# Attention probabilities left unscaled, 1/sum applied to the product with v, and transposes in two row tiles, in a fused attention, FFT, MLP and gate kernel

## The chip, the cores and the metric

The kernel runs on one core of one Trainium2 chip. The metric is the device time of one launch in microseconds (us); lower is better. The core's engines run side by side, each in its own order: PE (TensorE: matmuls, and PEld, its loads of the stationary operand), DVE (VectorE), ACT (ScalarE), POOL (GpSimd) and SP (SyncE, which here only issues DMAs). An instruction starts when the one before it on its engine has been issued and every semaphore that it waits for has come.

## The reference

Three blocks follow each other. The result of each is the x of the next.

```python
# 1: attention; batch 4, heads 8, seq 576, head_dim 64
scores = scale * q @ k.T
thresh = max(scores, -1) - tau                      # tau = 0.02
scores = where(scores >= thresh, scores, -1e9)
attn = exp(scores - max(scores))
attn = attn / (sum(attn, -1) + 1e-9)
x = attn @ v                                        # heads side by side: 4 x 576 x 512
# 2: mixing and MLP
u  = x + real(fft(fft(x, axis=1), axis=2))
un = (u - mean(u)) / sqrt(var(u) + 1e-6)
x  = u + relu(un @ w_ch1) @ w_ch2                   # 512 -> 2048 -> 512
# 3: gate
gate = sigmoid(causal depthwise convolution of x, 5 taps)
out = (gate * (x @ w_val)) @ w_out                  # 512 -> 512 -> 512
```

All inputs are 4-byte floats, except that the MLP and gate weights arrive as 8-byte words and are turned into two 4-byte parts each on the chip.

## The kernel before

**Attention.** Two heads form a head pair p; there are 16, and the 576 queries of the pair's two heads make nine tiles of 128 rows: four of each head (h = 0 or 1, i = 0 to 3) and one (h = 2) with the last 64 queries of both. So there are 144 tiles, numbered g, and 72 pairs of tiles, numbered u. One tile goes through these steps, each on one engine (`g_tile`):

- PE: scores `s` (L651). The head dimension is 64, so only half of the array's rows is needed: the upper 64 rows work out 288 keys and the lower 64 rows the other 288, as two *row tiles* whose matmuls run beside each other. Queries `qt` therefore lie twice, on partitions 0 to 63 and 64 to 127.
- DVE: minus the row maximum, `neg` (L716); once for two tiles the threshold `thr` (L661).
- ACT: the exponential `e` (L722).
- DVE: `p` (L733), which keeps the exponentials of scores over the threshold and sums them into `su`.
- ACT adds 1e-9 to the sums (L666) and DVE takes 1/sum (L668), once for two tiles; POOL multiplies `p` by it (L741).
- PE: four transposes of 128x128, `t` (L753), into one PSUM bank; there are two such banks (`ps_t`). The last 64 keys of each tile go through `g_tail` (L678, L682) into a bank of another pool.
- ACT: copies `t` to `m` (L770).

When a group of tiles of a pair is there, PE multiplies by v (L431, `f`), ACT copies the product to `xt` (L436), and the FFT's folds and matmuls follow after every fourth pair.

**Weights.** The MLP's weights come in 40 pieces of 128x512 words. POOL issues the loads into `raw` buffers (L903), then DVE (L261, L262, L265, L266, L267), ACT (L263, L264, L270) and POOL (L271) turn a piece into its high and low part. These conversions fill gaps of the attention and go on during the MLP's first chunk (chunk 0), in which `h` (L1216) and `c` (L1252) are the matmuls, ACT makes `hh` (L1228) and DVE `hl` (L1230). Chunks 1 to 4 (L1062, L1078) and the gate (L1450, L1468) follow.

**Order.** Nothing is ordered at run time. A planner in the program, `loom`, runs all these steps as generators against written costs (the second value of each `yield`, in ns), ranks (the third; a lower one is more urgent) and rooms (buffers), and emits each engine's instructions in the order that comes out of its own clock. A changed cost or rank thus moves instructions everywhere.

Of the kernel before, what the change touches and what calls it, by code (L numbers as in the profile page):

```python
# [32 lines left out]
GVF = 4  # L33
XB = 2
PBUFS = 6
# [7 lines left out]
HOLD = {"PE": 200.0, "DVE": 200.0, "ACT": 200.0, "POOL": 200.0}  # L43
# [7 lines left out]
SWAP = 350.0  # L51
# [25 lines left out]
class Loom:  # L77
# [222 lines left out]
def attention_fft(tc, right, ps_f, a, u_d, dram, conv_w, loom):  # L300
# [3 lines left out]
    with ExitStack() as right2, ExitStack() as right2b, ExitStack() as right3, ExitStack() as right4, ExitStack() as scores, ExitStack() as turned:  # L304
# [29 lines left out]
        ths = [[const.tile([128, n], F32, name=f"th{i}_{n}") for n in (256, 320)] for i in range(2)]  # L334
# [70 lines left out]
        def pt_tile(p, c):  # L405
            if (p, c) not in pt:
                pt[p, c] = (pt0_p, pt1_p)[c].tile([128, 2, 4, 256] if c == 0 else [128, 4, 640], F32, tag=f"m{c}", name=f"m{c}")
            return pt[p, c]

        def g_pv(p, c):  # L410
# [11 lines left out]
            for t in range(5):  # L422
# [217 lines left out]
        sc, neg, thr, ex, ssum, p_t = {}, {}, {}, {}, {}, {}  # L640
# [23 lines left out]
        def g_sum(u):  # L664
            yield "ACT", 210.0, 0.2
            ACT.activation(ssum[u], ssum[u], AF.Copy, bias=1e-9)  # L666
            yield "DVE", 155.0, 0.0
            DVE.reciprocal(ssum[u], ssum[u])  # L668
            loom.mark("r", u)

        def g_tail(p, rows):
            for j, i in enumerate(rows):
                yield ("PE", 112.0 if i < 4 else 120.0, 0.4, "full" if i < 4 else "col", *(["room"] if j == 0 else []))
                if j == 0:
                    f, room = fill_tile()
# [12 lines left out]
            ACT.activation(th[:, o:o + n], f[:, 0:n], AF.Copy)  # L688
# [3 lines left out]
        def g_tile(g):  # L692
            p, h, i = tiles[g]
            u, j = divmod(g, 2)
            c = 0 if i < 2 else 1
            yield "after", ("kq", p), *([("s", g - 1)] if g else []), *([("k", g - 2)] if g > 1 else [])
# [940 lines left out]
```

## Time and profile before

| what | value |
|---|---|
| median of 3 runs | 857.98 us (856.91 to 858.8) |
| the profiled execution: time, span of its instructions | 858.75 us, 857.0 us |
| mean granted TensorE clock, share of full speed | 0.992 |
| attention's loop: first `neg` to last `p` on DVE | 6.66 to 323.78 us |
| chunk 0 of the MLP: first `hl`, last `hl` on DVE; end of the chunk | 339.27, 434.73; 438.06 us |
| chunks 1 to 4 of the MLP | 438.06 to 751.05 us |
| gate and output | 751.05 us to the end |

The time of an execution is 1.75 us more than the span, which goes from its first instruction to its last. Busy times of different engines overlap, so they don't add up to the span. A stage is bound by the engine that is hardly idle in it, or by a chain that goes round several engines.

### The profile page before, as it was taken

What the parts mean: (1) busy time and instruction counts of PE and PEld (TensorE: products, weight loads), DVE (VectorE), ACT (ScalarE), POOL (GpSimd) and SP (SyncE); (2) the same over time, 40 slices, a digit from 0 to 9 for tenths busy, and PEclk for the clock granted to TensorE, in tenths of its full rate; (3) what the DMA queues carried; (4) which work ended last, traced back from release to release, by engine and by line L of the source; (5) the groups of instructions that cost most, each with busy time, mean ns of one, the idle gap of its engine ahead of it and who ended that gap; (6) DMA issues with size and microseconds to landing.
All of it is one profiled execution on the core that took longest, in us unless ns stands there. A gap on an engine that the chain in (4) does not pass through costs nothing.

```text
span 857.0 us, 13874 instructions
## 1 busy us (share of the span) xinstructions
PE 824.7 (96%) x4886; PEld 650.6 (76%) x4886; DVE 560.2 (65%) x1212; ACT 420.3 (49%) x855; POOL 384.7 (45%) x450
## 2 busy tenths in 40 slices
PE   6999999999999999999999999999999999999998
PEld 4555556656665656788889999998888788898986
DVE  6999999998988987797757632142123656328740
ACT  4877777787867765644545323133121331133432
POOL 3456974797588657574352431023003010075421
PEclk6999999999999999999999999999999999999999
DMA  7359455636754369959435622003000230532111
GB/s 213 101 155 244 131 144 155 190 121 208 203 168 144 102 205 334 376 197 365 151 124 179 212 65 60 0 28 108 1 1 12 93 105 1 194 122 90 62 50 62
DMA packets 63885, 117.37 MB, mean 137 GB/s; under 512 B 14658, under 2 KB 21826, under 8 KB 63816
## 3 DMA queue, kind: packets, MB, share of 16 engines
q1 hardware_dynamic: 56280, 92.62, 33.9%
q0 software_dynamic: 7104, 23.57, 9.0%
q8 instruction: 39, 0.64, 0.3%
q10 hardware_dynamic: 432, 0.30, 0.1%
q14 instruction: 30, 0.25, 0.1%
HBM read 84.99 MB, written 31.47 MB: 136 GB/s over the span
## 4 chain that ended last, share of the span: by engine, by line
PE 62%; DVE 17%; POOL 6%; issue 6%; ACT 5%; DMA 3%; SPq 0%; DVEq 0%; POOLq 0%; ACTq 0%
PE c L1078 15%; PE h L1062 14%; DVE neg L716 6%; DVE p L733 5%; PE o L1468 5%; PE h L1216 5%; PE v L1450 5%; PE s L651 5%; PE c L1252 4%; PE f L431 4%; PE t L753 3%; ACT e L722 2%; POOL p L741 2%; POOL res L1087 1%; PE f L563 1%
## 5 line engine op out<-in xcount | busy, mean ns | idle before, releaser
L741 POOL TENSOR_SCALAR p<-p,su 128x576 f32<-128x576 f32 x144 | 111.6, 784 | 89.2 <-DVE su L668 76.8
L1066 DVE SCALAR_TENSOR_TENSOR hl<-h,hh 128x384 fp32r<-128x384 f32 (+1 forms) x64 | 39.8, 622 | 147.4 <-ACT hh L1065 145.7
L1065 ACT ACTIVATE hh<-h 128x384 fp32r<-128x384 f32 (+1 forms) x64 | 34.8, 544 | 200.7 <-PE h L1062 195.5
L722 ACT ACTIVATE e<-s,neg 128x576 f32<-128x576 f32 x144 | 103.7, 741 | 51.4 <-DVE neg L716 38.7
L733 DVE SCALAR_TENSOR_TENSOR p<-s,thr,e 128x576 f32<-128x576 f32 x144 | 113.3, 815 | 11.2 <-ACT e L722 2.6
L716 DVE TENSOR_REDUCE neg<-s 128x1 f32<-128x576 f32 x144 | 103.1, 747 | 11.1 <-PE s L651 10.1
L651 PE MATMUL s<-kt,qt 64*128 64x288 f32 (+1 forms) x640 | 100.7, 448 | 8.5 <-DVE p L733 5.9
L1078 PE MATMUL c<-hl,w1h 128*128 128x384 f32 (+1 forms) x256 | 92.9, 363 | 1.9 <-DVE hl L1066 1.9
L1078 PE MATMUL c<-hh,w1h 128*128 128x384 f32 (+1 forms) x256 | 92.6, 362 | 0.0
L1078 PE MATMUL c<-hh,w1l 128*128 128x384 f32 (+1 forms) x256 | 92.6, 362 | 0.0
L753 PE MATMUL t<-ident,p 128*128 128x128 f32 x536 | 83.9, 286 | 8.3 <-POOL p L741 4.0
L753 PEld LDWEIGHTS t<-ident,p 128*128 128x128 f32 x536 | 59.4, 143 | 38.3 <-POOL p L741 24.7
L651 PEld LDWEIGHTS s<-kt,qt 64*128 64x128 f32 (+1 forms) x640 | 47.2, 179 | 46.9 <-issue 19.7
L770 ACT ACTIVATE m<-t 128x512 f32<-128x512 f32 x134 | 76.1, 600 | 12.6 <-PE t L753 12.2
L431 PE MATMUL f<-m,v 128*64 128x320 f32 (+1 forms) x512 | 72.4, 413 | 0.9 <-ACT th L688 0.9
L1062 PE MATMUL h<-unh,w0h 128*128 128x384 f32 (+1 forms) x256 | 61.6, 362 | 0.0
L1062 PE MATMUL h<-unh,w0l 128*128 128x384 f32 (+1 forms) x256 | 61.6, 362 | 0.0
L1062 PE MATMUL h<-unl,w0h 128*128 128x384 f32 (+1 forms) x256 | 61.5, 362 | 0.0
L1087 POOL TENSOR_TENSOR res<-ht,res 128x512 f32<-128x512 f32 (+1 forms) x20 | 23.0, 1188 | 84.2 <-DVE ht L1086 84.2
L431 PEld LDWEIGHTS f<-m,v 128*64 128x64 f32 x512 | 32.7, 136 | 29.3 <-issue 8.7
L1078 PEld LDWEIGHTS c<-hl,w1h 128*128 128x128 f32 x256 | 48.1, 188 | 7.9 <-DVE hl L1066 2.9
L1078 PEld LDWEIGHTS c<-hh,w1l 128*128 128x128 f32 x256 | 48.0, 188 | 5.0
(262 smaller groups left out, 1676.6 us busy)
## 6 DMA issues: line engine op xcount, KB each, us to landing
raw<-in_moe_w_ch POOLq DMA_DIRECT2D x32, 512.0 KB, 6.1
qt<-in_q SPq DMA_DIRECT2D x30, 288.0 KB, 6.9
kt<-in_k SPq DMA_DIRECT2D x15, 432.0 KB, 4.6
ypad<-y_d SPq DMA_DIRECT2D x16, 288.0 KB, 4.4
out<-os SPq DMA_DIRECT2D x18, 256.0 KB, 2.0
v<-in_v SPq DMA_DIRECT2D x16, 256.0 KB, 3.1
e_h<-cx SPq DMA_DIRECT2D x16, 256.0 KB, 2.4
e_l<-ct SPq DMA_DIRECT2D x16, 256.0 KB, 2.1
```

The costliest lines, as they stand in the source:

```text
L431: PE.matmul(out=f[h * 64:h * 64 + 64, 0:n], lhsT=w, rhs=r, start=(t == 0), stop=(t == 4))
L651: PE.matmul(out=s[o, c, 0:HALF], lhsT=qt[w, hh, q], rhs=kt[w, 2 if h == 2 and hh else hh], start=True, stop=True)
L716: DVE.tensor_reduce(out=neg[u][:, j, 0:1], in_=sc[g][:, :, 0:HALF], axis=AX.XY, op=ALU.max, negate=True)
L722: ACT.activation(e, sc[g][:, :, 0:HALF], AF.Exp, bias=neg[u][:, j, 0:1], scale=1.0)
L733: DVE.scalar_tensor_tensor(out=p_view(g).rearrange("p (a b) -> p a b", a=2), in0=sc.pop(g)[:, :, 0:HALF], scalar=thr[u][:, j:j + 1], in1=e ...
L741: POOL.tensor_scalar(out=v, in0=v, scalar1=ssum[u][:, j:j + 1], scalar2=1.0, op0=ALU.mult, op1=ALU.mult)
L753: PE.matmul(out=f[:, t, :], lhsT=pv[:, t * 128:(t + 1) * 128], rhs=ident, is_transpose=True, start=(t == 0), stop=(t == 3))
L770: ACT.activation(o, fv, AF.Copy)
L1062: PE.matmul(out=f[:, 0:n], lhsT=ww[:, k * 128:(k + 1) * 128], rhs=x[:, k, 0:n], start=(i == 0), stop=(i == 3 * KB - 1))
L1078: PE.matmul(out=ch[c][o][:, 0:n], lhsT=ww[:, o * 128:(o + 1) * 128], rhs=x, start=(at_ == 0 and i == 0), stop=(at_ == FB - 1 and i == 2))
L1216: PE.matmul(out=f[:, 0:n], lhsT=ww[:, k * 128:(k + 1) * 128], rhs=x[:, k, 0:n], start=(i == 0), stop=(i == 3 * KB - 1))
L1450: PE.matmul(out=f[:, 0:HALF], lhsT=w[:, k, o * 128:(o + 1) * 128], rhs=x[:, k, s], start=(i == 0), stop=(i == 3 * KB - 1))
```

## The change

- `p` stays unscaled. The sums of a head pair go into one column block `ssum[p % 3]` of [128, 9]. Per pair three times (two rows of tiles, two more, the last) `g_tail` adds 1e-9 on ACT, takes 1/sum on DVE (48 reciprocals in place of 72), spreads it over 64 columns a head on POOL (`lt`, 32 copies and 16 multiplications of a constant), and turns it on PE beside the tails (64 transposes of 128x128 and 32 matmuls with `both`, all new). `th` is twice as wide: the tails, and 1/sum along the free axis. After ACT's copy of the product with v, POOL multiplies `xt` by the second half of `th`, 32 times. POOL's 144 multiplications of `p` are gone.
- The transposes of a tile are 8 matmuls of 64 rows (two row tiles) in place of 4 of 128 rows; those of two tiles follow each other into one `ps_t` buffer of two banks, of which there is one. `PBUFS`, the buffers of `p`, go from 6 to 5.
- `q` is written twice in DRAM (128 rows), so that one plain DMA on one queue loads it; the first pair's queries no longer go through ACT's queue. Two constants, `half` and `both`, are made on DVE ahead of the loop; `both` needs `ident` to be there.
- One more `raw` buffer for weights (`mlp_raw_top0`) from the stage "probs" on; the gate takes its four buffers from a list of the older ones.
- The planner's numbers: ROOMS, TURN, COPY, HOLD of ACT, SWAP, and the rank 1.2 for `g_unit`.

```diff
+TURN = 250.0
+COPY = 1.05
+ROOMS = {"room_t": 1}
...
-PBUFS = 6
+PBUFS = 5
...
-HOLD = {"PE": 200.0, "DVE": 200.0, "ACT": 200.0, "POOL": 200.0}
+HOLD = {"PE": 200.0, "DVE": 200.0, "ACT": 400.0, "POOL": 200.0}
-SWAP = 350.0
+SWAP = 300.0
...
-        ps_t = pool(turned, "ps_t", 2, space=PSUM)
+        ps_t = pool(turned, "ps_t", 1, space=PSUM)
+        ssum = [const.tile([128, 9], F32, name=f"su{i}") for i in range(3)]
-        ths = [[const.tile([128, n], F32, name=f"th{i}_{n}") for n in (256, 320)] for i in range(2)]
+        ths = [[const.tile([128, 2, n], F32, name=f"th{i}_{n}") for n in (256, 320)] for i in range(2)]
...
-            for j, q in enumerate((SP, second)):
-                q.dma_start(out=qt[j * 64:j * 64 + 64], in_=a["q"][b, n])
+            second.dma_start(out=qt, in_=a["q"][b, n])
...
+                yield "POOL", pool_ns(n), 0.3, "port"
+                POOL.tensor_tensor(out=x, in0=x, in1=th[:, 1], op=ALU.mult)
                 loom.mark("x", p, c)
...
-        def g_sum(u):
-            yield "ACT", 210.0, 0.2
-            ACT.activation(ssum[u], ssum[u], AF.Copy, bias=1e-9)
-            yield "DVE", 155.0, 0.0
-            DVE.reciprocal(ssum[u], ssum[u])
+        def g_tail(p, rows):
+            tail = rows[0] == 4
+            su = ssum[p % 3][:, 8:9] if tail else ssum[p % 3][:, 2 * rows[0]:2 * rows[0] + 4]
             yield "ACT", 210.0, 0.2
+            ACT.activation(su, su, AF.Copy, bias=1e-9)
+            yield "DVE", 155.0, 0.1
+            DVE.reciprocal(su, su)
+            yield "POOL", 250.0 if tail else 400.0, 0.1, "port"
+            lt = tmp_p.tile([128, 4, D], F32, tag="lt", name="lt", bufs=1)
+            if tail:
+                POOL.tensor_scalar(out=lt[:, 0:2], in0=half, scalar1=su, scalar2=1.0, op0=ALU.mult, op1=ALU.mult)
+            else:
+                POOL.tensor_copy(out=lt, in_=su.unsqueeze(2).to_broadcast([128, 4, D]))
...
+                for h in range(2):
+                    w = slice(h * 64, h * 64 + 64)
+                    PE.matmul(out=f[w, 64:128], lhsT=lt[:, h], rhs=both, start=True, stop=True)
...
+                for j in range(2):
+                    PE.transpose(f[:, 256 + j * 128:384 + j * 128], lt[:, 2 * j:2 * j + 2].rearrange("q h d -> q (h d)"), ident)
...
-            yield "after", ("r", u), *([("n", g - 1)] if g else [])
-            yield "POOL", 782.0, 0.1, "port"
-            v = p_view(g)
-            POOL.tensor_scalar(out=v, in0=v, scalar1=ssum[u][:, j:j + 1], scalar2=1.0, op0=ALU.mult, op1=ALU.mult)
-            yield "PE", 437.0, 0.5, "full", "room_t", "room"
+            gs = (g - 1, g) if h == 1 else (g,)
+            yield "PE", TURN * len(gs), 0.5, "row", "room_t"
...
-            for t in range(4):
-                PE.matmul(out=f[:, t, :], lhsT=pv[:, t * 128:(t + 1) * 128], rhs=ident, is_transpose=True, start=(t == 0), stop=(t == 3))
+                for t in range(4):
+                    for b in range(2):
+                        w = slice(b * 64, b * 64 + 64)
+                        PE.matmul(out=f[:, b, 4 * x + t], lhsT=pv[w, t * 128:(t + 1) * 128], rhs=ident[w, w], is_transpose=True, start=True, stop=True)
...
+        DVE.tensor_tensor(out=both, in0=ident[:, 0:D], in1=ident[:, D:128], op=ALU.add)
...
+                more_room("raw", "mlp_raw_top0", top)
```

In the instructions' order on each engine the following moves. Conversions whose last DVE step (L267, of the change L270) stands ahead of the attention's last `p`: 15 before, 5 with the change; from there to the first `hl`: 2 and 2; from the first `hl` to the last: 16 and 26; behind the last `hl`: 8 and 8. Of the single steps ahead of the last `p`, L261 goes from 16 to 7, L262 from 15 to 7, L265 and L266 from 15 to 6, L267 from 15 to 5, the reciprocals from 71 to 45. A `p` is followed by the next `neg` with no other instruction between them, or only a reciprocal, 20 times before and 54 times with the change.

DVE in the attention, with the `p` of the 53rd and 54th of the 144 tiles at the top, before (`p` is L733, `neg` L716):

```order
L733 SCALAR_TENSOR_TENSOR p,su<-s,thr,e 128x576 x2
L261 TENSOR_SCALAR cx<-raw 128x512
L668 RECIPROCAL su<-su 128x2
L262 TENSOR_SCALAR ct<-raw 128x512
L716 TENSOR_REDUCE neg_188<-s 128x1 x2
L661 TENSOR_REDUCE thr<-neg_188 128x2
L733 SCALAR_TENSOR_TENSOR p,su<-s,thr,e 128x576 x2
```

The same engine ten tiles on, around the `p` of the 65th and 66th tile, with the change (`p` is L751 now, `neg` L734):

```order
L734 TENSOR_REDUCE neg_190<-s 128x1
L676 RECIPROCAL su_181<-su_181 128x4
L734 TENSOR_REDUCE neg_190<-s 128x1
L667 TENSOR_REDUCE thr<-neg_190 128x2
L751 SCALAR_TENSOR_TENSOR p,su_182<-s,thr,e 128x576 x2
L734 TENSOR_REDUCE neg_191<-s 128x1 x2
L667 TENSOR_REDUCE thr<-neg_191 128x2
```

Where steps of a conversion stood between `p` and the next `neg`, often nothing stands there now. They stand in chunk 0 instead; DVE there, between two `hl` (L1230), before:

```order
L1230 SCALAR_TENSOR_TENSOR hl<-h,hh 128x512
L265 SCALAR_TENSOR_TENSOR cx<-raw,cx 128x512
L266 SCALAR_TENSOR_TENSOR raw<-raw,ct 128x512
L267 TENSOR_SCALAR raw<-cx 128x512
L261 TENSOR_SCALAR cx<-raw 128x512
L262 TENSOR_SCALAR ct<-raw 128x512
L1230 SCALAR_TENSOR_TENSOR hl<-h,hh 128x512
```

And with the change (`hl` is L1245; L264, L265, L268, L269 and L270 are the steps of a conversion):

```order
L1245 SCALAR_TENSOR_TENSOR hl<-h,hh 128x512
L264 TENSOR_SCALAR cx<-raw 128x512
L265 TENSOR_SCALAR ct<-raw 128x512
L264 TENSOR_SCALAR cx<-raw 128x512
L265 TENSOR_SCALAR ct<-raw 128x512
L268 SCALAR_TENSOR_TENSOR cx<-raw,cx 128x512
L269 SCALAR_TENSOR_TENSOR raw<-raw,ct 128x512
L270 TENSOR_SCALAR raw<-cx 128x512
L268 SCALAR_TENSOR_TENSOR cx<-raw,cx 128x512
L269 SCALAR_TENSOR_TENSOR raw<-raw,ct 128x512
L270 TENSOR_SCALAR raw<-cx 128x512
L1245 SCALAR_TENSOR_TENSOR hl<-h,hh 128x512
```

One conversion stood between these two `hl` before (elsewhere two), and with the change two stand between nearly all of them. PE in the attention, before (`t` is L753, `s` L651):

```order
L651 MATMUL s<-kt,qt 128x288 x2
L651 MATMUL s<-kt,qt 64x288 x4
L753 MATMUL t<-ident,p 128x128 x4
L563 MATMUL f<-csh,aeh 128x290
L678 MATMUL f<-ident,p 128x128 x2
L753 MATMUL t<-ident,p 128x128 x4
```

And with the change (`t` is L766, `s` L657, the turned 1/sum L698):

```order
L657 MATMUL s<-kt,qt 64x288 x4
L766 MATMUL t<-ident,p 128x64 x16
L657 MATMUL s<-kt,qt 128x288 x2
L556 MATMUL f<-sdh,xoh 95x256 x2
L556 MATMUL f<-sdl,xoh 95x256 x2
L696 MATMUL f<-ident,p 128x128 x2
L698 MATMUL f<-ident,lt 128x128 x2
```

Four transposes of 128 columns became eight of 64 for a tile, and those of two tiles stand together, beside scores, which use row tiles too.

## Rows read from the trace of the kernel before

**Rows 1.** The page's first part: busy time of each engine, share, instructions.

```profile
PE 824.7 (96%) x4886; PEld 650.6 (76%) x4886; DVE 560.2 (65%) x1212; ACT 420.3 (49%) x855; POOL 384.7 (45%) x450
```

**Rows 2.** Windows: us, busy (count) of PE, PEld, DVE, ACT, POOL, PEclk, DMA share, GB/s.

```profile
6.66:323.78 317.12, 297.59 (x2164) 186.81 (x2161) 286.95 (x691) 236.34 (x513) 216.04 (x274) 0.98 0.58 166
323.78:438.06 114.28, 110.71 (x557) 89.14 (x556) 88.85 (x135) 59.98 (x114) 61.99 (x70) 1.00 0.74 262
438.06:751.05 312.99, 311.10 (x1552) 279.72 (x1552) 131.87 (x241) 85.76 (x149) 59.32 (x55) 1.00 0.25 81
```

**Rows 3.** Attention, DVE by line: count | busy, mean ns | idle before, ended by.

```profile
L716 DVE TENSOR_REDUCE neg<-s 128x1 f32<-128x576 f32 x144 | 103.1, 747 | 11.1 <-PE s L651 10.1
L266 DVE SCALAR_TENSOR_TENSOR raw<-raw,ct 128x512 f32<-128x512 uint32 x14 | 11.7, 833 | 0.0
L668 DVE RECIPROCAL su<-su 128x2 f32<-128x2 f32 x71 | 11.2, 157 | 1.9 <-ACT su L666 1.7
L265 DVE SCALAR_TENSOR_TENSOR cx<-raw,cx 128x512 int32<-128x512 int32 x14 | 10.7, 767 | 0.0
L261 DVE TENSOR_SCALAR cx<-raw 128x512 int32<-128x512 int32 x15 | 7.9, 529 | 0.0
L262 DVE TENSOR_SCALAR ct<-raw 128x512 int32<-128x512 int32 x15 | 7.1, 474 | 0.0
L267 DVE TENSOR_SCALAR raw<-cx 128x512 int32<-128x512 int32 x14 | 6.2, 442 | 0.0
```

**Rows 4.** Timeline of DVE at 121.3 us: start, duration, instruction [idle before].

```profile
121.30 0.82 DVE L733 SCALAR_TENSOR_TENSOR p<-s,thr,e 128x576 f32<-128x576 f32 x1
...
122.05 0.81 DVE L733 SCALAR_TENSOR_TENSOR p<-s,thr,e 128x576 f32<-128x576 f32 x1
...
123.07 0.76 DVE L716 TENSOR_REDUCE neg<-s 128x1 f32<-128x576 f32 x1 [0.20 <-PE s L651]
```

**Rows 5.** First chunk, 323.78 to 438.06 us, DVE by line.

```profile
L265 DVE SCALAR_TENSOR_TENSOR cx<-raw,cx 128x512 int32<-128x512 int32 x18 | 16.1, 894 | 1.4 <-ACT cx L263 1.4
L266 DVE SCALAR_TENSOR_TENSOR raw<-raw,ct 128x512 f32<-128x512 uint32 x18 | 14.8, 820 | 0.3 <-ACT ct L264 0.3
L262 DVE TENSOR_SCALAR ct<-raw 128x512 int32<-128x512 int32 x18 | 14.5, 805 | 0.0
L261 DVE TENSOR_SCALAR cx<-raw 128x512 int32<-128x512 int32 x17 | 12.2, 717 | 0.9 <-ACT w0h L270 0.9
L267 DVE TENSOR_SCALAR raw<-cx 128x512 int32<-128x512 int32 x18 | 8.0, 446 | 0.0
```

**Rows 6.** Timeline of DVE: the first and the last `hl` of the 16 of chunk 0.

```profile
339.27 0.69 DVE L1230 SCALAR_TENSOR_TENSOR hl<-h,hh 128x512 fp32r<-128x512 f32 x1 [4.86 <-ACT hh L1228]
...
434.73 0.69 DVE L1230 SCALAR_TENSOR_TENSOR hl<-h,hh 128x512 fp32r<-128x512 f32 x1 [2.61 <-ACT hh L1228]
```

**Rows 7.** Timelines of DVE and of POOL in chunk 0, two stretches.

```profile
412.40 0.42 DVE L261 TENSOR_SCALAR cx<-raw 128x512 int32<-128x512 int32 x1
...
416.97 1.27 DVE L262 TENSOR_SCALAR ct<-raw 128x512 int32<-128x512 int32 x1
...
416.87 1.08 POOL L271 TENSOR_TENSOR w1l<-raw 128x512 fp32r<-128x512 f32 x1 [1.48 <-issue]
```

**Rows 8.** Timeline of PE at 105.5 us, then PE's weight loads of the attention by line.

```profile
105.55 1.09 PE L753 MATMUL t<-ident,p 128*128 128x128 f32 x8
106.57 1.24 PE L651 MATMUL s<-kt,qt 64*128 64x288 f32 x8
...
L753 PEld LDWEIGHTS t<-ident,p 128*128 128x128 f32 x528 | 58.5, 143 | 37.8 <-POOL p L741 24.7 <-issue 11.5 <-POOL xf L487 0.5
L651 PEld LDWEIGHTS s<-kt,qt 64*128 64x128 f32 x504 | 43.0, 191 | 39.7 <-issue 17.5 <-PE f L431 5.9 <-DVE p L733 4.4
```

**Rows 9.** The tile `ident`, 0 to 20 us: its load (duration ns, first and last start).

```profile
L786 SPq DMA_DIRECT2D ident<-in_ident x1: 590/590/590, 2.5 to 2.5; - x1
...
DMA to landing us min/median/max: 4.9/4.9/4.9
```

More of the change, by code (lines that the diff above doesn't have):

```diff
@@ L146, in start @@
         s = max(self.now[e], t.ready)
-        rooms = [(x, self.put.get(x, 0) - 2) for x in how if x.startswith("room")]
+        rooms = [(x, self.put.get(x, 0) - ROOMS.get(x, 2)) for x in how if x.startswith("room")]
         if rooms:
@@ L683, in g_tail @@
             for i in rows:
                 loom.mark("tailed", p, i)
-            o, n = (256, 64) if rows[0] == 4 else (0, 256)
             th = ths[p % 2][0 if rows[0] == 0 else 1]
-            yield "ACT", act(n), 0.3
-            ACT.activation(th[:, o:o + n], f[:, 0:n], AF.Copy)
+            o = 256 if tail else 0
+            yield "ACT", act(2 * n), 0.3
+            ACT.activation(th[:, :, o:o + n], f[:, 0:2 * n].rearrange("k (a q) -> k a q", a=2), AF.Copy)
             loom.free(room)
@@ L695, in g_tile @@
             c = 0 if i < 2 else 1
+            if g % 9 == 0 and p > 2:
+                yield "after", ("tailed", p - 3, 4)
             yield "after", ("kq", p), *([("s", g - 1)] if g else []), *([("k", g - 2)] if g > 1 else [])
@@ L711, in g_tile @@
                 if u >= 6:
-                    yield "after", ("n", 2 * u - 11)
-                thr[u], ssum[u] = (sm_p.tile([128, 2], F32, tag=nm, name=nm) for nm in ("thr", "su"))
+                    yield "after", ("k", 2 * u - 11)
+                thr[u] = sm_p.tile([128, 2], F32, tag="thr", name="thr")
             neg[u] = negs[u % len(negs)]
@@ new lines, in g_tile @@
+            m = pt_tile(p, c)
+            f, room = ps_t.tile([128, 2, 8, 64], F32, tag="t", name="t"), loom.room("room_t")
+            for x, y in enumerate(gs):
+                pv = p_view(y)[:, TAIL if tiles[y][1] == 1 else 0:]
+                for t in range(4):
+                    for b in range(2):
+                        w = slice(b * 64, b * 64 + 64)
+                        PE.matmul(out=f[:, b, 4 * x + t], lhsT=pv[w, t * 128:(t + 1) * 128], rhs=ident[w, w], is_transpose=True, start=True, stop=True)
+                loom.mark("t", y)
@@ L796, in attention_fft @@
                 DVE.tensor_copy(t[:, j, 1:2], atau)
+        half = const.tile([128, 2, D], F32, name="half")
+        both = const.tile([128, D], F32, name="both")
+        for h in range(2):
+            for x in range(2):
+                DVE.memset(half[x * 64:x * 64 + 64, h], float(x == h))
+        DVE.tensor_tensor(out=both, in0=ident[:, 0:D], in1=ident[:, D:128], op=ALU.add)
         loom.end = 8500.0
@@ L842, in mlp @@
         heads = [0, 0]
-        raws, spare = {}, {"raw": deque(), "cv": deque()}
+        raws, spare, kept = {}, {"raw": deque(), "cv": deque()}, set()
         at, loaded = [0], [0]
@@ L871, in used @@
         def used(j):
-            if more and nxt[0] + nxt[1] < FB:
+            if more and nxt[0] + nxt[1] < FB and all(ids[j, i] in stored for i in range(2)):
                 gone.append(j)
@@ L1098, in g_unit @@
             yield "after", *l0
-            yield "ACT", act(n), 3
+            yield "ACT", act(n), 1.2
             ACT.activation(uh[:, k, 0:n], z[:, k], AF.Copy)
-            yield "DVE", dve(n), 3, "port"
+            yield "DVE", dve(n), 1.2, "port"
             DVE.tensor_tensor(out=ul[:, k, 0:n], in0=z[:, k], in1=f32(uh[:, k, 0:n]), op=ALU.subtract)
@@ L1316, in start_gate @@
         def start_gate():
-            rooms = [spare["raw"].popleft() for _ in range(KB)]
+            rooms = [r for r in spare["raw"] if r in kept]
+            assert len(rooms) == KB
             ypad0 = [f32(r[0].tile([128, 512, 2], I32, tag="raw", name="ypad").rearrange("p a b -> p (a b)"))[:, 0:S + NK - 1] for r in rooms]
@@ L1605, in laid_out @@
     q, k, v = (x.reshape(B, NP, 2, S, D) for x in (q, k, v))
-    c = {"q": q.transpose(0, 1, 4, 2, 3).reshape(B, NP, D, 2, S)}
+    c = {"q": np.tile(q.transpose(0, 1, 4, 2, 3), (1, 1, 2, 1, 1))}
     k = np.stack([k[:, :, 0], np.roll(k[:, :, 1], TAIL, axis=-2), k[:, :, 1]], axis=2)
```

85 lines of the change are left out of this document (36 added, 49 removed).

## The prediction

> **What bounds the kernel now.** I read the page's busy shares first: PE is busy for 96% of the span, no other engine for more than 76% [rows 1]. That is a mean over stages, so the windows come next [rows 2]. In chunks 1 to 4 PE is busy 311.10 of 312.99 us, and in the gate stage, which the change's code leaves alone, nothing is gained either. In the attention PE is busy 297.59 of 317.12 us and DVE 286.95, both close to the whole, so neither alone sets the pace: the chain goes round scores, maximum, exponential, `p`. In chunk 0 PE is busy 110.71 of 114.28 us, DVE 88.85.
>
> Then DVE's groups in the attention [rows 3]: beside the maxima (0.747 us each) stand five steps of the weights' conversions and 71 reciprocals. What idle time `neg` meets is mostly PE's scores, 10.1 us in all. The timeline shows a pair of tiles: two `p` start 0.75 us apart, then the next `neg` starts 1.02 us after the second `p` [rows 4]. So where nothing stands between `p` and `neg`, 1.02 - 0.75 = 0.27 us stay open; where a conversion's step stands there, it uses up that gap.
>
> Times below are of the profiled execution, 858.75 us; it lies 0.8 us over the median of the runs, which I take off at the end. A measurement of this kernel can tell about 0.2%, 1.7 us, from no change.
>
> **Attention, DVE.** By the order 9 of L261, 8 of L262, 9 each of L265 and L266, 10 of L267 leave the stretch up to the last `p`, and 26 reciprocals. An instruction's start lies about 0.07 us nearer to the one before than the durations say (0.82 against 0.75) [rows 4]. So the removed work is 9 x 0.46 + 8 x 0.40 + 9 x 0.70 + 9 x 0.76 + 10 x 0.37 = 24.2 us and 26 x 0.087 = 2.3 us [rows 3]: -26.5. The gaps come back: 54 - 20 = 34 more direct successions at 0.27 us, +9.2. The 20 of before explain some 4 us of the 10.1 that `neg` waits for scores (0.20 each [rows 4]); the other 6 are scores that PE brings late, and with PE unloaded (below) I let them go: -6, bounds 0 and -6.
>
> At the start the constant `both` waits for `ident` ahead of the first `neg`. Its load starts at 2.5 and lands 4.9 us later, at 7.4 [rows 9], while the first `neg` started at 6.66 (the first window's bound [rows 2]): +0.7, and with q on one queue in place of two I take +1, bounds 0 and +2. Together -26.5 + 9.2 - 6 + 1 = **-22.3**, so some 295 us.
>
> **Attention, PE.** A tile's four transposes take 1.09 / 2 = 0.545 us [rows 8], and eight of 64 rows replace them. No row shows such a transpose. The nearest are the scores, which are row tiles too: eight matmuls of 288 columns in 1.24 us, 0.31 for two side by side; by columns a pair of 64 takes 0.069 and four pairs 0.28 us. Upper bound: each of the eight as dear as a full one now, 8 x 0.136 = 1.09. I take 0.28, since the scores' loads visibly run in twos: 504 of 191 ns are 96 us of durations in 43.0 us busy, against 76 in 58.5 for the full transposes [rows 8]. That takes 144 x 0.265 = 38 us off PE; 64 new transposes at 0.136 and 32 small matmuls, at most as much each, put 9 to 13 back. PE then needs 297.6 - 38 + 11 = 271 of 295 us. I count no gain beyond the 6 us above, because DVE, with 287 - 26.5 = 260 us of work and 54 gaps of 0.27 (15 us), fills 275 of the 295.
>
> The page on TensorE speaks against this edit. The Trainium skill ("TensorE: Matmul & The Clock Gate", "LDWEIGHTS (loading the stationary operand)") says that a load of the stationary operand costs by its columns and not by its rows, so half as high a tile saves nothing; by its figure of P/1.2 ns eight loads of 128 columns are an estimated 0.85 us a tile. By that PE would have 44 us more work where my sum has 38 less. The overlapped loads of the scores are this trace's answer to it; the rival on serial loads below prices the case from rows.
>
> **Attention, other engines.** POOL loses 144 multiplications and gets 48 spreads and 32 products; it was busy 216 of 317 us [rows 2] and nothing on it sets a tile's pace afterwards: `p` goes to PE straight. The sum's way (ACT, DVE, POOL, PE, ACT) is longer, but is wanted only by the product's scaling behind `xt`. ACT has the same 144 copies `m`, 24 fewer biases and `th` twice as wide; its 236 us [rows 2] stay under 295. One `ps_t` of two banks in place of two of one makes the transposes of the next two tiles wait for both copies; `p` has five buffers to wait in. I cost it at nothing; if it stops PE, scores are late next, which is the 6 us not gained.
>
> **From the last `p` to the first `hl`** (323.8 to 339.3 [rows 6]) the same folds stand and two conversions, as before: 0. The product's scaling on POOL adds about one operation to that tail, under 1 us.
>
> **Chunk 0.** From the first to the last `hl` are 434.73 - 339.27 = 95.5 us [rows 6], with 16 conversions before and 26 after. A conversion costs DVE there 0.894 + 0.820 + 0.805 + 0.717 + 0.446 = 3.68 us [rows 5], less 5 x 0.07, 3.33. Fifteen `hl` at 0.69 less 0.07 are 9.3. Of DVE's 88.85 us, 18 x 3.33 + 16 x 0.62 = 69.9 are these; of the other 19 I place two thirds, 13, between the two `hl` (an estimate; the 15 us of folds ahead hold the rest). So DVE needs 26 x 3.33 + 9.3 + 13 = 109 us, 13 over what PE takes now. The lower bound: L262 takes 1.27 us while POOL's L271 runs and L261 0.42 when it doesn't [rows 7]; a conversion of the attention cost 3.05 - 0.35 = 2.7 [rows 3], and 26 x 2.7 + 22 = 92.5 fit into 95.5. So the price lies between 0 and +13; I take **+9**, nearer to the row of this very stage, since two conversions now stand between most `hl` and their steps meet POOL's at least as often.
>
> **Behind chunk 0.** Eight conversions as before, PE bound: 0.
>
> **Sum.** -22.3 + 9 = -13.3; 858.75 - 13.3 = 845.4 and 0.8 less for the median: **845 us**.
>
> **Rivals.**
> - *Chunk 0 stays PE's* (17%): the conversions collide less and cost 2.7 us. Then only the attention's -22.3 counts: 858.0 - 22.3 = 836 us. For it: DVE idled 25 of 114 us there. Against it: 3.33 measured in the place.
> - *Chunk 0 gives everything back* (14%, slower). The break-even price of a conversion is (95.5 + 22.3 - 22.3) / 26 = 3.7 us; in chunk 0 their durations already sum to 3.68. With a raw buffer's next load waiting in POOL's order behind other work, DVE stands idle between pieces and the effective price passes that: at 4.0 us it is 26 x 4.0 + 22.3 - 95.5 = +31, and 858 - 22 + 31 = 867 us. Against it: three or more raw buffers are in flight.
> - *The row tiles' loads are serial* (5%, slower). A tile's transposes then take 1.09 us: PE needs 297.6 + 78.5 + 11 = 387 us, the attention 70 more than 317, with chunk 0's +9 about 937 us. It decides from 0.46 us a tile, where PE's work reaches 295 us, and the kernel is slower than before from about 0.55.
> - *The forecast* (64%), own range 838 to 853.
>
> **Range and chances.** Forecast and first rival fill 834 to 853; of the second, cases just over break-even lie up to 860. I give 831 to 859. Faster: 64 + 17 and a little of the second rival, 0.83; same 0.05, slower 0.12.
>
> **What would show it.** Right: first `neg` to last `p` takes near 295 us with DVE busy over 88% of it; two tiles' transposes take about 0.56 us; `neg` waits less for `s`; from the first to the last `hl` 100 to 108 us, with `hl` waiting for DVE's conversions and PE's `c` for `hl`. Wrong: transposes over 0.45 us a tile; the attention shortened by much more than 22 us (then the late scores, not DVE's work, set the pace); or chunk 0 at 95 us, or over 115 with DVE idle and waiting for raw loads.

## The result and the profile after

The changed kernel takes 867.4 us (median, 866.63 to 868.41) beside 857.48 us: 1.011 times the time before, 95% interval 1.0098 to 1.0122. The forecast was 845 us, 831 to 859; the kernel is slower by 1.1%, and above the range.

The page's first part, of the changed kernel, answers to [rows 1]:

```profile
PE 815.5 (94%) x5590; PEld 644.2 (74%) x5590; DVE 566.7 (65%) x1193; ACT 427.5 (49%) x838; POOL 325.5 (38%) x386
```

PE works 9 us less than before in a span that is 9 us longer. Where it idles is in the windows (columns as in [rows 2]). Of the changed kernel these are the attention, the stretch to the first `hl`, the first six steps from `hl` to `hl` of chunk 0, the last nine, and the chunk's end:

```profile
6.96:298.93 291.97, 268.73 (x2792) 172.32 (x2792) 260.06 (x615) 225.44 (x462) 126.06 (x182) 0.98 0.44 142
298.93:314.56 15.63, 12.93 (x117) 9.16 (x115) 11.60 (x22) 8.59 (x20) 12.51 (x13) 1.00 0.86 279
314.56:383.20 68.64, 57.62 (x290) 44.97 (x286) 51.90 (x70) 32.38 (x65) 48.44 (x56) 0.92 0.80 266
383.20:445.44 62.24, 55.39 (x216) 40.31 (x216) 54.77 (x95) 35.71 (x61) 30.94 (x29) 0.97 0.44 146
445.44:448.76 3.32, 3.30 (x13) 2.45 (x14) 3.32 (x7) 1.62 (x4) 0.08 (x1) 1.00 0.01 2
```

The same two parts of chunk 0 before the change, six steps and nine:

```profile
339.27:382.70 43.43, 41.92 (x224) 35.69 (x223) 36.77 (x48) 25.27 (x51) 30.88 (x35) 1.00 0.84 303
382.70:434.73 52.03, 51.36 (x227) 42.18 (x225) 38.93 (x67) 25.43 (x43) 20.29 (x23) 1.00 0.63 223
```

The attention is 25.1 us shorter (291.97 against 317.12 [rows 2]), and the stretch behind it is as long as before. The 15 steps of chunk 0 take 130.9 in place of 95.5 us, +35.4: 25.2 in the first six, 10.2 in the last nine. Behind the chunk nothing moves by more than 2 us. So the loss is in chunk 0, and in neither half of it is PE's work alone the cause: PE is idle 11.0 us of the first part and 6.9 of the second, where it idled 1.5 and 0.7 before.

In the last nine steps PE's timeline shows how. Before the change, `c` (L1252) follows `h` (L1216) with no gap, because it is the `c` of the block before, whose `hh` and `hl` are long there:

```profile
408.52 1.07 PE L1216 MATMUL h<-unl,w0h 128*128 128x512 f32 x4
409.42 0.39 PE L1252 MATMUL c<-hh,w1h 128*128 128x512 f32 x1
```

With the change `h` (L1231) is followed by its own `c` (L1267):

```profile
394.28 1.07 PE L1231 MATMUL h<-unh,w0h 128*128 128x512 f32 x4
395.19 1.07 PE L1231 MATMUL h<-unh,w0l 128*128 128x512 f32 x4
396.09 1.07 PE L1231 MATMUL h<-unl,w0h 128*128 128x512 f32 x4
397.85 0.50 PE L1267 MATMUL c<-hh,w1h 128*128 128x512 f32 x1 [0.69 <-ACT hh L1243]
398.19 0.40 PE L1267 MATMUL c<-hh,w1l 128*128 128x512 f32 x1
```

In each such step PE waits 0.69 us for ACT's `hh`, and the first three `c` start 0.33 to 0.39 us apart in place of 0.23. A step takes 6.7 us where it took 5.45.

In the first six steps some of the weights themselves are late. Of PE's 11.0 us of idle time 5.7 are waits for a weight (`w0l`), 4.1 for operands of the FFT and of the mean (`sp`, `sm`, `boh`, `cs`) and 1.0 for `hh`:

```profile
PE h L1231 <- POOL w0l L274: 5.0, 1, 5.0
PE f L556 <- ACT sp L534: 1.6, 1, 1.6
PE f L569 <- DVE sm L597: 1.3, 1, 1.3
```

PE's timeline at 371 us shows the longest of them:

```profile
370.87 1.07 PE L1231 MATMUL h<-unh,w0h 128*128 128x512 f32 x4
376.98 1.22 PE L1231 MATMUL h<-unh,w0l 128*128 128x512 f32 x2 [5.04 <-POOL w0l L274]
```

And POOL's in the same stretch:

```profile
372.12 1.95 POOL L1126 TENSOR_TENSOR cs<-z 128x384 f32<-128x384 f32 x2
374.15 1.33 POOL L1128 TENSOR_TENSOR cs<-cs 128x384 f32<-128x384 f32 x1
375.44 1.49 POOL L274 TENSOR_TENSOR w0l<-raw 128x512 fp32r<-128x512 f32 x1
```

The low part of a weight comes 5 us after PE could have used it. The clock follows: ten-us windows from 358 us on, of the changed kernel.

```profile
358.00:368.00 10.00, 8.99 (x35) 6.23 (x35) 4.42 (x10) 4.38 (x9) 4.85 (x6) 0.94 0.90 300
368.00:378.00 10.00, 4.96 (x20) 3.76 (x19) 10.00 (x9) 2.56 (x5) 9.54 (x10) 0.91 0.81 266
378.00:388.00 10.00, 8.58 (x23) 5.93 (x22) 9.41 (x18) 5.33 (x11) 4.08 (x6) 0.57 1.04 389
```

PE is busy 4.96 of 10 us, and in the ten us behind that the granted clock is 0.57 of full speed on the mean, so for most of it at the lower of its two levels (1.2 of 2.4 GHz). Counted over the first six steps, a matmul of `h` took 275 ns from start to start in place of 228. The rest of the 25.2 us is for the most part work that came along: matmuls other than `h` and `c` are 141 (20.4 us) in place of 91 (12.2 us). Of the 50 more, 18 are the FFT's and 32 the last products with v (L434), which all stood ahead of the first `hl` before.

### The profile page after: what moved, and what is told of

The parts are those of the page before. It is cut to its first block, busy times and chain, and to the rows that moved or that the text cites. A ratio compares the mean times of both kernels' runs of the same rounds, so it can differ in the third digit from the quotient of the medians.

```text
span 866.1 us, 15062 instructions
## 1 busy us (share of the span) xinstructions
PE 815.5 (94%) x5590; PEld 644.2 (74%) x5590; DVE 566.7 (65%) x1193; ACT 427.5 (49%) x838; POOL 325.5 (38%) x386
## 4 chain that ended last, share of the span: by engine, by line
PE 71%; DVE 11%; issue 6%; POOL 4%; DMA 3%; ACT 3%; SPq 0%; POOLq 0%; DVEq 0%; ACTq 0%
PE c L1093 16%; PE h L1077 16%; PE s L657 9%; PE f L434 7%; PE o L1485 5%; PE v L1467 4%; PE h L1231 3%; DVE p L751 3%; PE c L1267 3%; PE t L766 3%; DVE neg L734 3%; PE f L569 2%; DMA xd<-xs 1%; DVE cx L268 1%; POOL res L1102 1%
## 5 line engine op out<-in xcount | busy, mean ns | idle before, releaser
L657 PE MATMUL s<-kt,qt 64*128 64x288 f32 (+1 forms) x640 | 108.9, 453 | 21.3 <-DVE p L751 13.7
L740 ACT ACTIVATE e<-s,neg 128x576 f32<-128x576 f32 x144 | 105.7, 742 | 45.9 <-DVE neg L734 30.0
L734 DVE TENSOR_REDUCE neg<-s 128x1 f32<-128x576 f32 x144 | 107.5, 755 | 21.6 <-PE s L657 18.8
L751 DVE SCALAR_TENSOR_TENSOR p<-s,thr,e 128x576 f32<-128x576 f32 x144 | 113.1, 813 | 7.7 <-PE f L696 0.3
L777 ACT ACTIVATE m<-t 128x512 f32<-128x512 f32 x144 | 83.4, 598 | 16.0 <-PE t L766 15.7
L657 PEld LDWEIGHTS s<-kt,qt 64*128 64x128 f32 (+1 forms) x640 | 46.1, 181 | 56.4 <-issue 23.5
L434 PE MATMUL f<-m,v 128*64 128x320 f32 (+1 forms) x512 | 73.8, 417 | 0.0
L766 PEld LDWEIGHTS t<-ident,p 64*128 64x128 f32 x1152 | 49.6, 142 | 16.7 <-ACT m L777 5.6
L766 PE MATMUL t<-ident,p 64*128 64x64 f32 x1152 | 52.0, 228 | 0.8 <-ACT m L777 0.4
L1093 PEld LDWEIGHTS c<-hh,w1l 128*128 128x128 f32 x256 | 48.1, 188 | 5.0
L1093 PEld LDWEIGHTS c<-hh,w1h 128*128 128x128 f32 x256 | 48.1, 188 | 4.9
L434 PEld LDWEIGHTS f<-m,v 128*64 128x64 f32 x512 | 32.7, 138 | 24.6 <-issue 8.6
```

The source lines that it names most:

```text
L434: PE.matmul(out=f[h * 64:h * 64 + 64, 0:n], lhsT=w, rhs=r, start=(t == 0), stop=(t == 4))
L657: PE.matmul(out=s[o, c, 0:HALF], lhsT=qt[w, hh, q], rhs=kt[w, 2 if h == 2 and hh else hh], start=True, stop=True)
L734: DVE.tensor_reduce(out=neg[u][:, j, 0:1], in_=sc[g][:, :, 0:HALF], axis=AX.XY, op=ALU.max, negate=True)
L740: ACT.activation(e, sc[g][:, :, 0:HALF], AF.Exp, bias=neg[u][:, j, 0:1], scale=1.0)
L766: PE.matmul(out=f[:, b, 4 * x + t], lhsT=pv[w, t * 128:(t + 1) * 128], rhs=ident[w, w], is_transpose=True, start=True, stop=True)
L777: ACT.activation(o, f[:, :, 4 * x:4 * x + 4], AF.Copy)
```

## The experiments

Four theories were at hand. A: DVE's put-off conversions set chunk 0's pace. B: PE's order of `h` and `c` does. C: the folds' DMA round trips, or POOL's order behind them, do. D: the change's own operations do. Every version is compared by the time from the first to the last `hl`, split after six steps as above, but in e8 after seven (columns of [rows 2]). Pieces are counted in the traces, without the convolution's small one: by L267 or L270, 14 were done before the last `p` before the change, 4 with it. Some expectations count the small one too (15 and 5, and 14 for what is 12).

**e1_thin.** The same order, less DVE work:

```diff
-V.scalar_tensor_tensor(out=x, in0=high, ..., in1=x, ...)
+V.scalar_tensor_tensor(out=x[:, 0:16], in0=high[:, 0:16], ..., in1=x[:, 0:16], ...)
...
-V.tensor_scalar(out=high, in0=x, ...)
+V.tensor_scalar(out=high[:, 0:16], in0=x[:, 0:16], ...)
```

> The changed kernel with the same order of instructions on every engine; three of the five DVE steps of each weight conversion (L268, L269, L270) work on 16 columns in place of 512, and POOL's last step multiplies another operand. Left out: most of the conversion, so the weights are other numbers. In the changed kernel the first hl to the last hl takes 130.9 us, and these three steps cost there 0.83 + 1.01 + 0.57 us for each of 25 pieces. Theory A (DVE's conversion work sets chunk 0's pace): some 50 us of DVE work go there, PE's own work of 113 us becomes the limit, and the stretch falls by 12 us or more; the kernel takes 846 to 856 us. Theory B (PE's order, where h stands right before its own c, so that PE waits for ACT and DVE in each step of 6.7 us): the stretch keeps its steps and falls by under 5 us; with up to 6 us less in the attention the kernel takes 857 to 864.

It took 860.58 us (one run).

```profile
313.21:376.70 63.49, 55.07 (x289) 43.33 (x285) 37.63 (x69) 32.26 (x65) 44.05 (x54) 0.98 0.80 270
376.70:438.49 61.79, 55.61 (x216) 40.43 (x216) 32.23 (x95) 34.79 (x61) 26.71 (x30) 0.97 0.49 168
```

DVE is busy 32 of 61.8 us in the last nine steps, not 55 of 62.2, and they last as long: 6.7 us each. A alone falls. The first six gained 5.2, so the whole stretch is 5.6 us shorter, a little over the 5 that B allowed.

**e2_ahead.** The order alone, by one condition of the planner:

```diff
             yield "after", ("hl", j), ("placed", ids[j, 1]), *([("c", j - 1)] if j else [])
+            if j > 3 and j + 1 < FB:
+                yield "after", ("h", j + 1)
```

> The changed kernel with one more condition in the planner: the c of block j (j over 3) comes after the h of block j + 1, so PE has h's matmuls to run while ACT and DVE make hh and hl. The conversions stay where they are. Theory A (DVE's conversion work paces chunk 0): within 3 us of the changed kernel's 867. Theory B (PE's order): the 0.69 us wait for hh and the 0.56 us of slower c go from about 11 steps, 12 to 14 us less: 853 to 856.

865.7 us, 1.0081 times the kernel before (1.0064 to 1.0099).

```profile
315.66:385.40 69.74, 56.12 (x281) 44.71 (x278) 52.24 (x70) 32.26 (x65) 48.48 (x56) 0.88 0.77 258
385.40:443.12 57.72, 52.41 (x217) 39.58 (x217) 55.55 (x94) 35.66 (x61) 30.25 (x29) 1.00 0.50 163
```

The last nine gained 4.5 us, not 12, and now DVE is busy 55.55 of 57.72 us. B alone falls too.

**e5_thin_ahead.** Both edits in one.

> Both edits before this in one: three DVE steps of each conversion on 16 columns, and c of block j after h of block j + 1. Left out: most of the conversion, so the weights are other numbers. With the thin steps alone the last nine steps from hl to hl took 6.7 us each, with the order alone 6.4 on the mean, before the change 5.4. Theory (two limits side by side in chunk 0, DVE's conversions and PE's order, so that taking away one leaves the other): these steps fall to 5.4 to 5.7 us, and the kernel takes 846 to 853 us. Rival (a third limit behind both: the raw loads or POOL's last step of a conversion): the steps stay over 6.2 and the kernel over 856.

850.2 us (one run).

```profile
310.69:375.50 64.81, 54.67 (x281) 43.64 (x278) 38.34 (x68) 32.20 (x65) 44.19 (x54) 0.95 0.79 270
375.50:426.59 51.09, 49.69 (x218) 40.43 (x217) 33.97 (x95) 34.72 (x61) 26.70 (x30) 1.00 0.58 195
```

The last nine steps take 51.1 us, less than the 52.0 before the change: -0.4 by one edit, -4.5 by the other, -11.1 by both. That shows two limits side by side. The first six stay at 64.8, so they have another cause: PE waits 5.1 us for one `w0l` there, as in the changed kernel.

**e9_lo_dve.** As e5, with a conversion's last step on DVE, away from POOL's order:

```diff
-ops.append(("P", lambda: nc.gpsimd.tensor_tensor(out=lo(), ...)))
+ops.append(("P", lambda: V.tensor_tensor(out=lo(), ...)))
```

> As the run with thin steps and the c of block j after the h of block j + 1, and POOL's last step of each conversion (L274) is given to DVE, at the same place of the program. Left out, as there: most of the conversion. There the first six steps of chunk 0 still took 64.8 us (43.4 before the change), with POOL idle for 6.5 us ahead of a fold (L601) that waits for a DMA, and PE idle for 5.1 us until a last step of a conversion behind it on POOL. Theory (in this stretch the conversions wait behind the folds in POOL's order): the first six steps fall by 5 us or more, the kernel to 841 to 846 us. Rival (the raw loads, which stay on POOL's queue, or DVE's own order set it): the six steps stay within 3 us and the kernel at 848 to 853.

855.56 us (one run), with an attention 4 us longer than in e5.

```profile
315.54:379.80 64.26, 54.82 (x280) 43.31 (x277) 37.69 (x78) 32.38 (x65) 35.70 (x45) 0.93 0.80 267
```

The first six steps didn't move, as the rival had it, though the kernel lies over the rival's 853: the last step's place on POOL alone isn't what makes the weights late there. PE's longest wait for a weight in these steps is now 3.2 us for a DMA (`w0h<-e_h`), which brings a converted piece back from DRAM.

**e3_hold.** Conversions back into the attention, by one planner number:

```diff
-HOLD = {"PE": 200.0, "DVE": 200.0, "ACT": 400.0, "POOL": 200.0}
+HOLD = {"PE": 200.0, "DVE": 400.0, "ACT": 400.0, "POOL": 200.0}
```

> The changed kernel with one planner number changed: DVE work of low rank may hold up a tile's step by 400 in place of 200 of the planner's ns. By the order 14 conversions are done before the last p in place of 5 (15 before the change). Theory A: nine conversions at 2.7 us go back into the attention, where they refill open gaps: 10 to 20 us more there; chunk 0 loses nine at 3.4 us, 25 to 31 less: 848 to 860 us. Theory B (PE's order in chunk 0, which is still h before its own c at the chunk's end): chunk 0 shortens by less than 12 and the kernel takes 865 to 875. A third theory, that chunk 0 is long because of the last folds' DMA round trips ahead of it and not for the conversions, also gives 865 to 875.

856.68 us, 0.9984 (0.9972 to 0.9996); 12 pieces done before the last `p`.

```profile
7.52:308.50 300.98, 269.21 (x2820) 172.96 (x2821) 277.35 (x656) 237.61 (x482) 141.10 (x199) 0.98 0.52 166
323.19:375.20 52.01, 47.95 (x253) 39.45 (x247) 24.22 (x43) 23.48 (x48) 30.28 (x37) 1.00 0.84 296
375.20:433.55 58.35, 53.16 (x217) 41.11 (x217) 47.22 (x80) 29.99 (x52) 28.09 (x30) 0.97 0.67 240
```

Eight pieces cost the attention 9.0 us and gave chunk 0 back 20.5, of which 16.6 in the first six steps; theory A had nine pieces, 10 to 20 and 25 to 31. In the first six steps PE waits for no weight now, and DVE has half its work. The last four steps (the next expectation says five) are still 6.7 us each, with the 0.69 us wait.

**e7_hold_ahead.** e3 with e2's condition.

> The changed kernel with the planner's DVE number at 400 and c of block j after h of block j + 1; by the order 12 conversions are done before the last p. With 400 alone the last five steps still took 6.7 us with PE waiting 0.69 us in each. If DVE has room there now, these steps fall to 5.5 us, 5 to 7 us less: 849 to 853 us. If the conversions still set the pace, 855 to 858.

852.95 us, 0.9938 (0.9918 to 0.9957); 12 pieces.

```profile
324.01:369.80 45.79, 45.79 (x248) 38.78 (x244) 25.13 (x44) 23.55 (x47) 25.09 (x31) 1.00 0.92 330
369.80:427.76 57.96, 51.99 (x216) 40.92 (x215) 47.87 (x79) 29.63 (x52) 33.48 (x35) 0.97 0.64 229
```

The time is in the range of the theory, but not for its reason. The last nine steps, where it looked for 5 to 7 us, take 57.96 us in place of 58.35: PE waits 3.7 us there for the mean's operand and 2.2 for weights. The 6.2 us came in the first six steps. PE isn't idle for a moment in these, with the last folds still beside them, so theory C falls as a limit of its own: the folds' round trips cost PE nothing where it has other matmuls to go on with. The kernel is faster than before the change, by 0.6%.

**e6_hold600.** The same number at 600.

> The changed kernel with the planner's DVE number at 600 in place of 200: by the order 16 conversions are done before the last p (5 in the change, 15 before it), and PE's order in chunk 0 has h ahead of c again. Theory (conversions left for chunk 0 are what lengthened it): attention 305 to 312 us, first to last hl 95 to 102, the kernel 845 to 853 us, so most of what the row tiles and the unscaled p gave shows. Rival (the attention loses as much as chunk 0 gets back): 856 or more.

857.11 us, 0.9988 (0.9972 to 1.0003), outside what the theory gave and in the range of its rival (856 or more); 16 pieces.

```profile
7.08:325.21 318.13, 277.96 (x2829) 177.88 (x2829) 285.54 (x673) 242.94 (x490) 151.54 (x207) 0.96 0.54 171
385.70:435.86 50.16, 49.90 (x219) 40.84 (x219) 35.27 (x66) 23.52 (x43) 21.64 (x21) 1.00 0.52 182
```

Chunk 0 is as good as before (97.7 us in all, the last nine 50.2), as expected; the attention is not, at 318 us where 305 to 312 were expected: four more pieces than in e3 cost it 17, over 4 us each. `neg` waits 23.9 us for scores there, the clock is 0.96, and which of the moved instructions does it wasn't tried.

**e8_before_defer.** The kernel before the change, with its DVE number at 0 in place of 200.

> The kernel before the change, with one planner number changed: DVE work of low rank may hold up a tile's step by 0 in place of 200 of the planner's ns. By the order 8 conversions are done before the last p in place of 15. Theory (putting conversions off lengthens chunk 0 by more than it shortens the attention, whatever else changes): attention 5 to 14 us shorter, first to last hl 20 to 30 longer, 864 to 880 us. Rival (chunk 0 is long in the changed kernel for something that the change brings, the product's scaling on POOL or the longer way of the sums): 850 to 860.

875.27 us (one run); 8 pieces before the last `p`.

```profile
7.95:309.27 301.32, 284.01 (x2104) 179.79 (x2102) 269.06 (x659) 226.86 (x497) 199.23 (x258) 1.00 0.53 151
321.42:386.30 64.88, 58.22 (x291) 44.68 (x286) 40.87 (x56) 26.92 (x54) 35.98 (x42) 0.95 0.89 306
386.30:449.19 62.89, 53.67 (x237) 40.67 (x236) 55.39 (x89) 33.60 (x60) 35.05 (x36) 1.00 0.70 253
```

Without anything of the change's code the old kernel shows as long a chunk 0: 127.8 us from the first to the last `hl`, 32.3 more than before, where the changed one has 130.9. Only the total can be compared: the last two rows are split after the seventh step, and after six, as elsewhere, the parts are 49.8 and 78.0 us, since the last fold comes later here. The signs are the same, in other places: PE waits 5.8 us for a late weight (`w0h<-e_h`), its `c` waits 4.2 us for `hh`, and 54 products with v come behind the first `hl`. The attention is 15.8 us shorter for six pieces fewer, 2.6 each. Both moved a little further than the theory gave. Theory D isn't needed for chunk 0. The planner's number moves all of DVE's work of low rank, so what is shown is the effect of putting work off in this planner, not of the conversions by themselves.

**e4_full.** Full transposes in the changed order:

```diff
...
-for b in range(2):
-    PE.matmul(out=f[:, b, 4 * x + t], lhsT=pv[w, t * 128:(t + 1) * 128], rhs=ident[w, w], ...)
+PE.matmul(out=f[:, x, t], lhsT=pv[:, t * 128:(t + 1) * 128], rhs=ident, ...)
...
```

> The changed kernel with full 128x128 transposes again (4 a tile, into the same two-bank buffer, in the same order on every engine); everything else as in the change. If row tiles run in twos as the sum has it (0.28 us a tile against 0.545), PE gets 38 us back in the attention, passes DVE there, and the attention grows by 15 to 25 us: 880 to 893. If row tiles save nothing on PE or PE's time is not wanted there, within 4 us of 867.

900.45 us (one run), 7 over the upper bound.

```profile
7.16:328.65 321.49, 301.14 (x2234) 184.84 (x2234) 260.16 (x615) 227.04 (x462) 125.71 (x182) 0.99 0.40 128
```

PE has 32.4 us more work in the attention (301.14 against 268.73) and the attention is 29.5 longer: in this order, which was planned for the cheaper transposes, nearly every us of PE's is wanted.

**e11_no_raw.** The change without its additional raw buffer.

```diff
-                more_room("raw", "mlp_raw_top0", top)
```

> The changed kernel without the additional raw buffer for weights (mlp_raw_top0). If the raw loads set the pace of the conversions in chunk 0, as the rival of the prediction had it, the kernel takes 873 us or more; if DVE and PE's order set it, within 4 us of 867.

878.92 us (one run), 11.5 more.

```profile
382.60:456.43 73.83, 61.53 (x216) 43.14 (x216) 55.47 (x97) 35.73 (x61) 33.61 (x30) 0.90 0.42 137
```

That is the first branch of the expectation. The last nine steps take 73.8 us with DVE busy 55.5 of them, as much as in the changed kernel, and PE waits 4.0 us for `w0l` in them, where it waited for none. But no step on DVE waits for a raw load in chunk 0, here or in the changed kernel. A buffer less also changes the planner's order, so that raw loads are the limit here isn't shown; that the buffer is worth 11.5 us is.

**e10_swap.** e7 with SWAP as it was before.

```diff
-SWAP = 300.0
+SWAP = 350.0
```

> The version with the planner's DVE number at 400 and c of block j after h of block j + 1 (852.95 us), with SWAP at 350 as it was before the change. By the order 12 conversions are done before the last p, as in that version. If the number of conversions and the order of h and c are what counts, 850 to 856 us; if the order in the attention, which SWAP moves, counts as much, it lies outside.

849.28 us, 0.9891 (0.9863 to 0.992), a little under the range given.

```profile
7.29:306.59 299.30, 269.98 (x2833) 174.15 (x2835) 276.21 (x655) 236.66 (x482) 142.41 (x199) 0.99 0.51 164
320.19:369.70 49.51, 46.39 (x246) 38.87 (x245) 30.91 (x47) 23.81 (x49) 32.23 (x39) 1.00 0.86 302
369.70:422.68 52.98, 50.18 (x215) 39.44 (x214) 50.66 (x79) 29.83 (x51) 30.98 (x30) 1.00 0.69 249
```

It lies too near the range, with runs from 846.76 to 851.49 us, to tell whether the order in the attention counts as much. It beats both kernels: the attention is 17.8 us shorter than before, and chunk 0 7.0 longer.

**e12_delay.** e10 with three planned landing times cut (those of the FFT's constants, a fold's and the raw pieces; the expectation misnames the first).

```diff
-                    yield "delay", 8000.0
+                    yield "delay", 5500.0
```

> The version with the planner's DVE number at 400, SWAP 350 and c of block j after h of block j + 1 (849.28 us), with three loads (values, a fold's and the weights' raw pieces) planned to land after 5500 in place of 8000 of the planner's ns; the raw loads' median landing measured in chunk 0 of the changed kernel is 5.4 us. By the order 11 conversions are done before the last p, and h stands ahead of c nearly throughout. If conversions planned nearer to when their data lands come earlier on the chip too, 843 to 849 us; if the order of DVE then waits for late loads, 851 or more.

852.34 us, 0.9927 (0.9904 to 0.9949). The time is that of the second branch, but not its reason: DVE waits 0.8 us for a raw load in chunk 0, 4.8 for a stored piece's DMA (`e_h<-cx`) and 7.5 for PE's `f`. The chunk took 108.5 us and the attention 302.6; a plan nearer to one measured landing wasn't a better order.

## Why the prediction was wrong

**The attention's number was right, in part by luck.** It was to end 22.3 us earlier and ended 24.8 earlier: 25.1 us shorter, begun 0.3 us later, where 0 to 2 was put. DVE's work fell by 26.9 us (286.95 to 260.06), where 26.5 was put. `neg` waited 10.1 us for scores before, and now 18.8 (in all, how often, the longest):

```profile
DVE neg L716 <- PE s L651: 10.1, 22, 2.0
DVE neg L734 <- PE s L657: 18.8, 62, 1.6
```

These +8.7 us are the gaps between `p` and `neg` that came back, put at +9.2: 57 of the 62 waits are under 0.5 us. The -6 for late scores didn't come: waits of over 0.6 us were 6.5 us in all before and are 4.5 now. In its place the rest of DVE's idle time (ahead of `p`, the folds and the reciprocals) fell by 7.0 us, from 20.1 to 13.1, which no term of the sum had. That this made up for it is luck.

The row tiles' transposes were put at 0.28 us a tile; two tiles take 0.59 us from start to start in the changed kernel, 0.295 each:

```profile
108.19 0.66 PE L766 MATMUL t<-ident,p 64*128 64x64 f32 x16
108.78 0.72 PE L657 MATMUL s<-kt,qt 64*64 64x288 f32 x8
```

PE needed 268.7 us, not 271. The saving was put at 38 us, too much: 0.545 us for a tile's full transposes is half a duration, whose end lies over the next start. From start to start eight take 1.02 us (105.55 to 106.57 [rows 8]), 0.51 a tile, and 144 x (0.51 - 0.295) are 31 us. e4 shows the term from the other side: 32.4 us of PE's work go with the row tiles.

**The step that failed is the sum for chunk 0, +9.** It took the longer of DVE's work (109 us) and PE's pace before (95.5) as the most that the stretch could last, and +9 of these 13. DVE's work was sized well: it is busy 106.7 us there, and a conversion costs it 1.01 + 0.83 + 0.73 + 0.57 + 0.55 less 5 x 0.07, 3.34 us, where 3.33 was put:

```profile
L269 DVE SCALAR_TENSOR_TENSOR raw<-raw,ct 128x512 f32<-128x512 uint32 x26 | 26.3, 1011 | 0.0
L268 DVE SCALAR_TENSOR_TENSOR cx<-raw,cx 128x512 int32<-128x512 int32 x25 | 20.7, 829 | 0.5 <-ACT cx L266 0.5
L265 DVE TENSOR_SCALAR ct<-raw 128x512 int32<-128x512 int32 x25 | 18.2, 727 | 0.2 <-DMA e_l<-ct 0.2
L270 DVE TENSOR_SCALAR raw<-cx 128x512 int32<-128x512 int32 x26 | 14.8, 571 | 0.0
L264 DVE TENSOR_SCALAR cx<-raw 128x512 int32<-128x512 int32 x25 | 13.7, 548 | 0.2 <-DMA e_h<-cx 0.2
```

But the stretch took 130.9 us, +35.4 where +9 was put. A maximum over engines holds only while the one isn't waiting for the other, and three things broke that, none of which the sum looked at. First, PE's order in chunk 0 had changed as well: `h` stood right before its own `c`, which costs PE 1.25 us a step whatever DVE does (e1, e2, e5). This order goes with the work put off: PE's `c` waits 6.5 us for `hh` in chunk 0 with 4 pieces done before the last `p`, 4.3 with 12 (e3), not at all with 16 (e6), and 4.2 in the old kernel with 8 (e8). Second, pieces put off were such as the first blocks need: PE idled 11.0 us in the first six steps, 5.7 of them for weights, and part of its clock went (e3, e6 and e8 show that how much is put off decides it). Third, the first six steps took in 50 other matmuls more. The prediction showed DVE's order in chunk 0 and took PE's for granted.

**The rivals.** The slower one gave 867 us, and 867.4 were measured, but for another reason: it had a conversion cost DVE 4.0 us, with raw loads waiting. They cost 3.34, and no step on DVE waits for a raw load in chunk 0; what e11 shows is that without the added buffer it would be longer still. Serial loads of row tiles fall with the 0.295 us, and a chunk 0 that stays PE's with its 35.4 us more. (The 0.46 us a tile from which serial loads would decide is 0.45 by the rival's own terms, 0.28 + 24 / 144; nothing hangs on it.)

**What stays open.** Which step of a late conversion is the last one in the first six steps: not DVE's three wide ones (e1, e5), not POOL's place for the last alone (e9). The DMAs of the converted pieces are the nearest that wasn't tried. Nor is it settled what unscaled probabilities are worth by themselves. With 12 pieces done the changed attention takes 299 to 302 us; the old one would by e8's 2.6 us a piece take 312, so the change itself is worth some 10 to 13 us there, and at 16 pieces (318 against 322) 4. At the change's own 4 pieces the same estimate, carried further than any run of the old kernel went, gives 291 where 292 was measured: by it all of the 25.1 us come from the pieces put off, as in the prediction's sum, and the row tiles only made up for what the rest of the change cost. So it depends on the order; no run has the one without the other.

## What to carry to other kernels

When a planner puts fill work off, its price in the next stage isn't the larger of two engines' sums: read the order of the waiting engine there too, and ask for which consumer the put-off pieces are the first input. A stage with two limits side by side shows neither of them when one alone is taken away, so take both away in one run. After a change that frees an engine in one stage, look at whether fill work still finds its gaps there: two planner numbers and one condition turned 1.1% slower into 1.1% faster.

## What the runs showed of the hardware

Sixteen transposes of 64 rows on two row tiles took 0.59 us for two tiles from start to start, against 1.02 for eight full ones [rows 8]. A single load of half the height is not shorter, 142 ns on the mean against 143 [rows 8], but they overlap: 1112 loads of 142 ns are 158 us of durations in 48.1 us busy, where the 528 full ones were 76 in 58.5 [rows 8].

```profile
L766 PEld LDWEIGHTS t<-ident,p 64*128 64x128 f32 x1112 | 48.1, 142 | 15.5 <-ACT m L777 4.7 <-issue 1.7 <-ACT xt L440 1.0
```

The Trainium skill ("TensorE: Matmul & The Clock Gate", "LDWEIGHTS (loading the stationary operand)") has a load cost by its columns alone. The 142 and 143 ns agree with that; adding up a tile's eight loads in sequence, to an estimated 0.85 us, is what the 0.295 us measured contradict. The 0.295 us agree with the same page's section "The mechanism", by which loads overlap with matmuls of another row group.

An idle PE cost more than its idle time: after ten us in which it was busy 4.96, the granted clock was 0.57 over the next ten.
